# A fused attention, soft mixture and gated mixture: the second mixture's tiles laid out anew, its first loads in the other order, the last expert's additions on another engine

## The chip, the core and the metric

One core of a Trainium2 chip runs the whole program in one launch. The engines work side by side, each through its own queue in order: TensorE (PE, with PEld for its weight loads), VectorE (DVE), ScalarE (ACT) and GpSimd (POOL); SyncE (SP) issues the DMAs. The metric is the device time in microseconds (us); lower is better. TensorE runs at one of two granted clocks, 1.2 or 2.4 GHz, and the profile gives the granted share (0.5 or 1.0).

## The reference

```python
x = attn(q, k, v, M_prev, z_prev, beta)        # (2304, 512): local causal softmax mixed with a memory read
# first mixture: 8 experts, 4 slots each
d = softmax(x @ phi, axis=0); slots = d.T @ x
for e in range(8): slot_out[e] = relu(slots[e] @ w1[e]) @ w2[e]
x = softmax(x @ phi, axis=1) @ slot_out         # c @ slot_out, rank 32
# second mixture: 8 experts over all 2304 rows
P = exp(x @ w_gate - max); 8 times: P /= rows' sums, P /= columns' sums, P *= N / 8
out = sum over e of P[:, e:e+1] * (relu(x @ w1[e]) @ w2[e])
```

All inputs and outputs are float32.

## The kernel before

Attention runs first (its pairs of heads one after another), with the routing of the first mixture beside it. The first mixture follows (lines 762 to 861): its 32 weight pieces `wm` of 1 MB each are loaded by SP into ten `big`, four `bg2` and eight `wb` buffers; PE multiplies the slots with them (line 830, layer 1; line 848, layer 2, into `pso`), and lines 854 to 860 copy and turn `pso` into `soT`, the 32 slot outputs. `hT` is the hidden layer that line 848 reads as weights of PE.

The second mixture never forms x. x is `c @ slot_out`, so the first layer of expert e becomes `c4T` (the combine weights, times P for that expert) times `A_e = slot_out @ w1[e]`. `prepare_a` (line 986) makes A from the loaded `w1`; `split_a` cuts it into a rounded part `ahi` and a remainder `alo`; `spread_a` (line 1009) multiplies these by the selection matrix `sel` so that each slot row stands where the 128-row layer-1 matmul wants it; `store_a` writes the result to `a4`. Every product of the second mixture is done in three matmuls, high by high, high by low and low by high, to keep float32 accuracy.

The rows are cut into nine units of 256, so that there are 72 steps: eight experts of nine units. The first six units of expert 0 are multiplied in the plain way (`plain`, line 1316: 128x512 matmuls). All other 66 steps use seven products instead of eight on 2x2 blocks (Winograd's form): line 1344, `product`, each of 12 matmuls of 128x256, in the order p5, p1, p7, p6, p2, p3, p4. In a product the hidden tile (`a11h`, `s1l`, ...) is loaded as PE's weights and the weight tile (`BB1h`, `T2l`, ...) streams past it. The two combined hidden tiles come from DVE (line 1059), ACT rounds them (line 1065), POOL or DVE makes the remainders (lines 1076, 1072). DVE adds the products from PSUM into `accA`, `accB`, `accD` (line 1370). `layer1` (line 1030, eight matmuls, `l<-c4T,a`) of the next unit stands between the second product and the third; its PSUM banks are free when DVE has read `a22l` of the unit before (line 1072).

For each expert the weights are prepared beside the products of the expert before (`w_sum`, `w_hi`, `w_lo`, lines 936 to 968). For expert 0 that happens ahead: `load_w1(0, 1)` and then `load_raw(0)` (lines 1400, 1401) queue four 0.5 MB loads each on SP, and in the stretch with a written order (lines 1411 on) ACT rounds the raw second layer to `BB1h`, `BB2h` and POOL makes `BB1l`, `BB2l`; then come `prepare_a`, `gate_slots` (which repeats `soT` four times into `soB` for the gate), `split_a`, `spread_a`, `store_a`, `layer1`. `sel` is made by a DVE `tensor_scalar` (line 972) and three DVE casts of `ident` (line 978); these stand outside the written order and are placed by the scheduler.

At the last expert `add_u` (line 1252) adds the shared part U, kept in `accA[:, :256]`, to `accB` and `accD`, both on DVE, right behind the collection of p2; each finished block is sent out by SP as soon as it is final.

The tiles are laid one after another in the order in which they are first asked for, each rounded up to 32 bytes, pool behind pool: `mA`, `mB`, `mC`, `mD`. Counted from the first byte of `mA` and taken by 512 bytes, which is where `c4T` starts too, the tiles begin at:

| tile | before | after the change |
|---|---|---|
| BB1, T1 and T2 of even experts, c4T | 0 | 0 |
| T1, T2 of odd experts, T4, BB2, raw | 192 | 0 |
| a11, a12, a22, a21 and s3 (one tile) | 64 | 64 |
| s1, s2, s4 | 192 | 64 |
| a4 | 160 | 64 |

`rr` (72 bytes) and `cs` (32) stand ahead of `cP`, `chi`, `f` and `s1`, `s2`, `s4` in `mB`; that is where the 128 bytes between 64 and 192 come from. `sel` at the start of `mD` lies over the second `hT`, whose last reader is the last matmul of line 848.

Of the kernel before, what the change touches and what calls it, by code (L numbers as in the profile page):

```python
# [8 lines left out]
F32 = mybir.dt.float32  # L9
BF16 = mybir.dt.bfloat16  # L10
F32R = mybir.dt.float32r
AF = mybir.ActivationFunctionType
# [9 lines left out]
def infini_attention_soft_moe_sinkhorn_moe(  # L22
# [848 lines left out]

    mA = ctx.enter_context(tc.tile_pool(name="mA", bufs=1, reuse_waits="tile"))
    mB = ctx.enter_context(tc.tile_pool(name="mB", bufs=1, reuse_waits="tile"))
    mC = ctx.enter_context(tc.tile_pool(name="mC", bufs=1, reuse_waits="tile"))
    mD = ctx.enter_context(tc.tile_pool(name="mD", bufs=1, reuse_waits="tile"))
    ps_l = ctx.enter_context(tc.tile_pool(name="ps_l", bufs=1, space=PSUM, reuse_waits="tile"))
# [91 lines left out]
        )  # L968


    sel = mD.tile([P, 4, 160], F32R, name="sel")
    nc.vector.tensor_scalar(
        out=sel.rearrange("p j c -> p (j c)"), in0=ones[:, 0:1].to_broadcast([P, 640]),
# [2 lines left out]
    for r in (0, 2, 4):  # L976
# [1 line left out]
        nc.vector.tensor_copy(  # L978
            sel[:, :, 32 * r : 32 * r + 32], ident.rearrange("p (j s) -> p j s", j=4)
        )  # L980
    a2s, a4s, G = {}, {}, {}

    def aux(nm):
        return ps_a.tile([P, 512], F32, tag="a", name=nm)
# [13 lines left out]
    def split_a(e):  # L998
        pa = a2s[e]
        ahi = mB.tile([P, 256], F32R, tag="ahi", name="ahi")  # L1000
        nc.scalar.activation(out=ahi, in_=pa[:, 0:256], func=AF.Copy)
        alo = mB.tile([P, 256], F32R, tag="alo", name="alo")
        nc.vector.tensor_tensor(
            out=alo, in0=pa[:, 0:256], in1=ahi.bitcast(F32), op=ALU.subtract
        )
        a2s[e] = ahi, alo
        a4s[e] = mD.tile([P, FF], F32R, tag="a4", name="a4", bufs=2)

    def spread_a(e, n):

# [97 lines left out]

    soR = soT.rearrange("p c (o s) -> p c o s", o=1)
    Pr = mB.tile([P, NTT, E], F32, name="Pr")  # L1110
    Cw = mD.tile([P, NTT, NS], F32, name="Cw")

    gsel = mD.tile([P, E + NS], F32R, name="gsel")
    m1 = mD.tile([P, 1], F32, name="m1")
    m2 = mD.tile([1, 1], F32, name="m2")

    def gate_slots():
        soB = G["soB"] = mB.tile([P, KD, 4, NS], F32, tag="c4", name="soB")
        for c in range(KD):
            nc.vector.tensor_copy(soB[:, c], soR[:, c].to_broadcast([P, 4, NS]))  # L1120

    def gate_weights():
        pg, soB = aux("pg"), G["soB"]
# [46 lines left out]
        nc.scalar.activation(out=Pr, in_=Pr, func=AF.Exp, bias=m1)  # L1170

    def balance_rows():
        rr = mB.tile([P, NTT], F32, tag="rr", name="rr")
        nc.vector.tensor_reduce(out=rr, in_=Pr, op=ALU.add, axis=AX.X)
        nc.vector.tensor_scalar_add(rr, rr, 1e-9)
        nc.vector.reciprocal(rr, rr)
        nc.vector.tensor_tensor(
            out=Pr, in0=Pr, in1=rr.rearrange("p (t o) -> p t o", o=1).to_broadcast([P, NTT, E]),
            op=ALU.mult,
        )  # L1180
        cs = G["cs"] = mB.tile([P, E], F32, tag="cs", name="cs")
        nc.vector.tensor_reduce(
            out=cs, in_=Pr.rearrange("p t e -> p e t"), op=ALU.add, axis=AX.X
        )
# [67 lines left out]
    def add_u(u, g):  # L1252

        A, B_, D_ = accA[:, u], accB[:, u], accD[:, u]
        eng(g[0]).tensor_tensor(
            out=halves(B_), in0=halves(B_), in1=both(A[:, 0:CW]), op=ALU.add
        )
        eng(g[1]).tensor_tensor(out=D_, in0=D_, in1=A[:, 0:CW], op=ALU.add)
# [100 lines left out]
    def collect(g, k, y):  # L1359
        e, u = units[g]  # L1360
        nm = ORDER[k]

        A, B_, D_ = accA[:, u], accB[:, u], accD[:, u]
        new, end = e == 0, e == E - 1

        def put(acc, y, new=new):
            if new:
                nc.scalar.activation(out=acc, in_=y, func=AF.Copy)
            else:
                nc.vector.tensor_tensor(out=acc, in0=acc, in1=y, op=ALU.add)  # L1370

        def send(i, c, t):
            r0 = P * (2 * u + i)
            nc.sync.dma_start(out[r0 : r0 + P, CW * c : CW * c + CW], t)

        if nm == "p5":
            put(halves(B_), both(y))
        elif nm == "p1" and e == 1 and u < RAW:
            put(A[:, 0:CW], y, True)
            put(A[:, CW:], y)  # L1380
        elif nm == "p1":
            put(halves(A), both(y))
        elif nm == "p7":
            put(D_, y)
        elif nm == "p2":
            put(A, Y[g, "y3"], False)
            if end:
                send(0, 0, A[:, CW:])
                add_u(u, "DD")
        elif nm == "p3":  # L1390
            put(B_, Y[g, "y2"], False)
            if end:
                send(0, 1, B_[:, 0:CW])
                send(1, 1, B_[:, CW:])
        elif nm == "p4":
            put(D_, y, False)
            if end:
                send(1, 0, D_)

    load_w1(0, 1)  # L1400
    load_raw(0)
    BB.update({(2, z): mC.tile([P, KH, 2, CW], F32R, name=f"BB2{z}") for z in "hl"})
    EX = {}

# [5 lines left out]
    with tc.manual_schedule(engines={E_.PE, E_.DVE, E_.Activation, E_.Pool}):  # L1410
        for nm in ("B11", "B12", "B21", "B22"):
            for i in range(2):
                w_hi(0, nm, i)
                w_lo(0, nm, i, "P")
        prepare_a(0)
        gate_slots()
        split_a(0)
        spread_a(0, 0)
        spread_a(0, 1)
        store_a(0, 0)  # L1420
        store_a(0, 1)
        layer1(0)
        split_h(0, "a11")
        split_h(0, "a21")
        gate_weights()
        for g in range(len(units)):
            nxt = g + 1 < len(units)
            for k in range(7):
                s = 7 * g + k
                if g < RAW:  # L1430
                    plain(g, k)
                    if k == 3:
                        layer1(g + 1)
                    if k == 0:
                        if g:
                            store(g - 1, 2)
                        split_h(g, "a12")
                    elif k == 1:
                        split_h(g, "a22")
                    elif k == 6:  # L1440
                        store(g, 1)
                    if k > 3 and g == RAW - 1:
                        hidden(g + 1, k - 2)
                    elif k in (4, 5):
                        split_h(g + 1, ("a11", "a21")[k - 4])
                else:

                    EX[s + 1] = g, k, product(g, k)
                    if k == 1 and nxt:
                        layer1(g + 1)  # L1450
                    if g == RAW and k == 0:
                        store(g - 1, 2)
                        hidden(g, 5)
                        hidden(g, 6)
                    if k not in (3, 4):
                        result(s)
                    if k == 0:
                        hidden(g, 0)
                    elif k > 1 and nxt:
                        hidden(g + 1, k)  # L1460
                    result(s)
                for fn, args in side.pop(s, ()):
                    fn(*args)
        result(7 * len(units))
# [60 lines left out]
```

## Time and profile before

| | |
|---|---|
| device time, median of three runs | 1181.48 us (1179.54 to 1184.17) |
| profiled execution | 1182.51 us, of which the span from the first to the last instruction is 1180.7 us |
| busy | PE 1120.1 us (95%), DVE 865.7 (73%), ACT 656.3 (56%), POOL 641.8 (54%) |
| attention, first mixture, second mixture | 0 to 268 us, 268 to 316, 316 to the end |
| mean granted clock | 0.986 |

In the profile a line gives start, duration, engine, source line, operation, output<-inputs, shapes and, in brackets, how long the engine was idle before and who ended it. A PE matmul's own duration holds its way through the array; what one costs in a dense stream is the distance from its start to the next start.

### The profile page before, as it was taken

How to read it: one execution, taken by the hardware profiler on the slowest of the kernel's cores; microseconds unless marked ns; L12 is line 12 of the kernel's file. 1: busy time of each engine (PE TensorE's matmuls, PEld its weight loads, DVE VectorE, ACT ScalarE, POOL GpSimd, SP SyncE). 2: the span in 40 equal slices, each digit the busy share in tenths (PEclk: the TensorE clock that was granted, in tenths of full speed). 3: DMA queues.
4: the chain of work that ended last, by engine and by line, in shares of the span. 5: the costliest groups of instructions: out<-in, count | busy, mean ns of one | idle time of the engine just before them, and what ended most of it. 6: DMA issues, size and time to landing. Idle time of an engine off the chain costs nothing.

```text
span 1180.7 us, 24363 instructions
## 1 busy us (share of the span) xinstructions
PE 1120.1 (95%) x9247; PEld 1018.6 (86%) x9247; DVE 865.7 (73%) x1891; ACT 656.3 (56%) x1422; POOL 641.8 (54%) x585
## 2 busy tenths in 40 slices
PE   6899999979799999999999999999999999999998
PEld 4677777764287888999999999999999999999998
DVE  6888888874337566677778767777876777788886
ACT  6788888741233487546545644654564465456342
POOL 5433323200323297577677767767776776686443
PEclk9999999998989999999999999999999999999999
DMA  6677686249702004002100400210040031000111
GB/s 158 192 200 226 197 245 178 74 187 376 309 6 71 1 2 143 1 2 82 62 2 1 143 2 1 92 53 1 1 143 1 2 108 37 2 1 19 42 50 54
DMA packets 37412, 102.32 MB, mean 87 GB/s; under 512 B 6448, under 2 KB 13232, under 8 KB 33200
## 3 DMA queue, kind: packets, MB, share of 16 engines
q1 hardware_dynamic: 36864, 100.69, 26.5%
q8 instruction: 73, 1.20, 0.4%
q14 instruction: 43, 0.35, 0.1%
q10 hardware_dynamic: 432, 0.09, 0.0%
HBM read 96.04 MB, written 4.72 MB: 85 GB/s over the span
## 4 chain that ended last, share of the span: by engine, by line
PE 75%; DVE 11%; ACT 7%; DMA 3%; issue 2%; POOL 1%; SPq 0%; ACTq 0%; DVEq 0%; POOLq 0%
PE y L1356 16%; PE y L1354 16%; PE y L1355 16%; PE l L1035 6%; PE y L1321 5%; PE po L436 3%; PE pt L399 2%; ACT sm L360 2%; DMA wm<-in_moe_w_dram 1%; PE pa L992 1%; DVE sm L356 1%; PE pc L1221 1%; PE ph L830 1%; DVE f L1059 1%; DMA raw<-in_moe_w_dram 1%
## 5 line engine op out<-in xcount | busy, mean ns | idle before, releaser
L1059 DVE SCALAR_TENSOR_TENSOR f<-l,f 128x512 f32<-128x512 f32 x264 | 181.4, 687 | 56.6 <-ACT a11h L1065 44.4
L1076 POOL TENSOR_TENSOR s1l<-f,s1h 128x512 fp32r<-128x512 f32 x66 | 88.4, 1340 | 170.0 <-ACT s1h L1065 165.9
L1370 DVE TENSOR_TENSOR accA<-accA,y 128x512 f32<-128x512 f32 (+1 forms) x129 | 86.6, 671 | 57.1 <-PE y L1356 51.6
L1065 ACT ACTIVATE a12h<-l 128x512 fp32r<-128x512 f32 x72 | 43.1, 598 | 121.6 <-DVE f L1059 121.6
L1076 POOL TENSOR_TENSOR s4l<-f,s4h 128x512 fp32r<-128x512 f32 x66 | 86.0, 1303 | 39.9 <-ACT s4h L1065 39.8
L1370 DVE TENSOR_TENSOR accB<-accB,y 128x512 f32<-128x512 f32 x129 | 88.3, 684 | 13.7 <-PE y L1356 2.3
L1035 PE MATMUL l<-c4T,a 128*128 128x256 f32 x576 | 82.7, 286 | 9.2 <-DVE a22l L1072 8.3
L1076 POOL TENSOR_TENSOR s2l<-f,s2h 128x512 fp32r<-128x512 f32 x66 | 85.9, 1301 | 0.8 <-ACT s2h L1065 0.8
L1076 POOL TENSOR_TENSOR s3l<-f,s3h 128x512 fp32r<-128x512 f32 x66 | 86.0, 1303 | 0.3 <-ACT s3h L1065 0.3
L1035 PEld LDWEIGHTS l<-c4T,a 128*128 128x128 f32 x576 | 75.0, 190 | 12.4 <-DVE a22l L1072 10.8
L360 ACT ACTIVATE sm<-sm,mn 128x128 f32<-128x128 f32 (+3 forms) x128 | 71.1, 556 | 19.5 <-DVE mn L356 17.9
L965 POOL TENSOR_TENSOR BB1l<-raw,BB1h 128x512 fp32r<-128x512 f32 x32 | 41.0, 1293 | 68.9 <-ACT BB1h L959 68.9
L1354 PE MATMUL y<-T2h,s2h 128*128 128x256 f32 x264 | 76.9, 291 | 0.0
L1354 PE MATMUL y<-BB2h,a12h 128*128 128x256 f32 x264 | 75.0, 284 | 0.0
L1355 PE MATMUL y<-BB2l,s4h 128*128 128x256 f32 x264 | 74.6, 283 | 0.1
L1354 PE MATMUL y<-BB1h,a11h 128*128 128x256 f32 x264 | 73.4, 278 | 1.3 <-DVE accB L1370 1.3
L1356 PE MATMUL y<-T4h,a22l 128*128 128x256 f32 x264 | 74.6, 283 | 0.0
L1356 PE MATMUL y<-BB2h,a12l 128*128 128x256 f32 x264 | 74.5, 282 | 0.0
L1356 PE MATMUL y<-BB2h,s4l 128*128 128x256 f32 x264 | 74.5, 282 | 0.0
L1354 PE MATMUL y<-BB2h,s4h 128*128 128x256 f32 x264 | 74.5, 282 | 0.0
L1354 PE MATMUL y<-T4h,a22h 128*128 128x256 f32 x264 | 74.3, 281 | 0.0
L1356 PE MATMUL y<-T1h,s1l 128*128 128x256 f32 x264 | 74.1, 281 | 0.0
(313 smaller groups left out, 4219.0 us busy)
## 6 DMA issues: line engine op xcount, KB each, us to landing
wm<-in_moe_w_dram SPq DMA_DIRECT2D x32, 1024.0 KB, 7.7
w<-in_moe_w_dram SPq DMA_DIRECT2D x32, 512.0 KB, 4.4
raw<-in_moe_w_dram SPq DMA_DIRECT2D x32, 512.0 KB, 4.1
qd<-in_q_dram SPq DMA_DIRECT2D x30, 288.0 KB, 4.2
kd<-in_k_dram SPq DMA_DIRECT2D x30, 288.0 KB, 4.5
qp<-in_q_dram SPq DMA_DIRECT2D x16, 288.0 KB, 3.4
vt<-in_v_dram SPq DMA_DIRECT2D x16, 256.0 KB, 2.7
out_dram<-accB SPq DMA_DIRECT2D x18, 128.0 KB, 1.8
```

What stands on the lines that cost most here:

```text
L360: nc.scalar.activation(out=sm[:, 0:n], in_=sm[:, 0:n], func=AF.Exp, scale=-1.0, bias=mnc, accum_out=X.sums[:, i, h : h + 1],)
L436: nc.tensor.matmul(po[64 * h : 64 * h + 64, c0:w], X.vt[:, j, h, :], rhs, start=(j == 0), stop=(j == n - 1),)
L965: eng(g).tensor_tensor(out=w_tile(e, nm, "l")[:, h], in0=full(e, nm, i), in1=w_tile(e, nm, "h")[:, h].bitcast(F32), op=ALU.subtract,)
L1035: nc.tensor.matmul(ph[:, f, :], a4s[e][:, P * (KH * j + f) : P * (KH * j + f) + P], c4T[:, UT * u : UT * u + UT], start=True, stop=True,)
L1059: nc.vector.scalar_tensor_tensor(out=f_tile(g, nm), in0=ph(g, src), scalar=0.0, in1=b, op0=ALU.max, op1=op)
L1065: nc.scalar.activation(out=h_tile(g, nm, "h"), in_=ph(g, nm) if a else FU[g, nm], func=AF.Relu if a else AF.Copy)
L1076: nc.gpsimd.tensor_tensor(out=lo, in0=FU[g, nm], in1=hi, op=ALU.subtract)
L1321: nc.tensor.matmul(Y[g, i], X[g, f"a{i}{j}", "hhl"[n]][:, f, :], BB[j, "hlh"[n]][:, f].rearrange("p a c -> p (a c)"), start=j == 1 and f = ...
L1354: nc.tensor.matmul(o_, hh[:, f, :], wh[:, f, :], start=f == 0, stop=False)
L1355: nc.tensor.matmul(o_, hh[:, f, :], wl[:, f, :], start=False, stop=False)
L1356: nc.tensor.matmul(o_, hl[:, f, :], wh[:, f, :], start=False, stop=f == KH - 1)
L1370: nc.vector.tensor_tensor(out=acc, in0=acc, in1=y, op=ALU.add)
```

## The change

```diff
+    mS = ctx.enter_context(tc.tile_pool(name="mS", bufs=1, reuse_waits="tile"))
+    mS.tile([P, 24], F32, name="gap")
     mC = ctx.enter_context(tc.tile_pool(name="mC", bufs=1, reuse_waits="tile"))
...
+    mD.tile([P, 16], F32, name="gap")
+    a4s = {0: mD.tile([P, FF], F32R, tag="a4", name="a4", bufs=2)}
+    Cw = mD.tile([P, NTT, NS], F32, name="Cw")
     sel = mD.tile([P, 4, 160], F32R, name="sel")
...
-    gsel = mD.tile([P, E + NS], F32R, name="gsel")
-    m1 = mD.tile([P, 1], F32, name="m1")
-    m2 = mD.tile([1, 1], F32, name="m2")
+    gsel = mS.tile([P, E + NS], F32R, name="gsel")
+    m1 = mS.tile([P, 1], F32, name="m1")
+    m2 = mS.tile([1, 1], F32, name="m2")
...
-        for c in range(KD):
-            nc.vector.tensor_copy(soB[:, c], soR[:, c].to_broadcast([P, 4, NS]))
+        nc.scalar.activation(out=soB, in_=soR.to_broadcast([P, KD, 4, NS]), func=AF.Copy)
...
-        rr = mB.tile([P, NTT], F32, tag="rr", name="rr")
+        rr = mS.tile([P, NTT], F32, tag="rr", name="rr")
...
-        cs = G["cs"] = mB.tile([P, E], F32, tag="cs", name="cs")
+        cs = G["cs"] = mS.tile([P, E], F32, tag="cs", name="cs")
...
             if end:
                 send(0, 0, A[:, CW:])
-                add_u(u, "DD")
+                if u == NU - 1:
+                    add_u(u, "DP")
         elif nm == "p3":
             put(B_, Y[g, "y2"], False)
-            if end:
+            if end and u == NU - 1:
                 send(0, 1, B_[:, 0:CW])
                 send(1, 1, B_[:, CW:])
         elif nm == "p4":
             put(D_, y, False)
             if end:
+                if u < NU - 1:
+                    add_u(u, "PP")
+                    send(0, 1, B_[:, 0:CW])
+                    send(1, 1, B_[:, CW:])
                 send(1, 0, D_)
 
+    load_raw(0)
     load_w1(0, 1)
-    load_raw(0)
...
         prepare_a(0)
-        gate_slots()
         split_a(0)
         spread_a(0, 0)
         spread_a(0, 1)
         store_a(0, 0)
         store_a(0, 1)
+        gate_slots()
         layer1(0)
```

`rr` and `cs` leave `mB`, and the small pool `mS` (448 bytes) stands between `mB` and `mC`, which gives the third column of the table above. `sel` moves to the end of `mD`, above everything that the first mixture uses. `raw` takes the places that expert 0's `w1` had, and the other way round. In `add_u` the letters are the engines of the addition into `accB` and of that into `accD`: D for DVE, P for POOL. For the first eight units of the last expert both additions stand on POOL behind the collection of p4, and the three blocks are sent there; the ninth keeps its place behind p2, with the second addition on POOL.

## Rows read from the trace of the kernel before

**Rows 1.** Waits of TensorE, 427 to 1181 us: total, times, longest.
```profile
PE l L1035 <- DVE a22l L1072: 7.8, 10, 1.7
```
**Rows 2.** The same view, 470 to 1082 us: the whole answer.
```profile
PE pa L992 <- ACT c4T L1226: 0.2, 1, 0.2
```
**Rows 3.** The waits of all engines, 1082 to 1166 us, the last expert.
```profile
PE l L1035 <- DVE a22l L1072: 3.7, 7, 0.6
PE y L1354 <- DVE accB L1370: 1.3, 1, 1.3
```
**Rows 4.** Timeline of PE, one unit of expert 5: each product's first matmul.
```profile
913.81 0.28 PE L1354 MATMUL y<-T1h,s1h 128*128 128x256 f32 x1
...
917.58 0.28 PE L1354 MATMUL y<-BB1h,s3h 128*128 128x256 f32 x1
918.96 0.28 PE L1354 MATMUL y<-T2h,s2h 128*128 128x256 f32 x1
920.40 0.28 PE L1354 MATMUL y<-BB2h,a12h 128*128 128x256 f32 x1
...
924.68 0.28 PE L1354 MATMUL y<-T1h,s1h 128*128 128x256 f32 x1
```
**Rows 5.** The same, one unit of expert 6.
```profile
1016.31 0.28 PE L1354 MATMUL y<-T1h,s1h 128*128 128x256 f32 x1
...
1021.43 0.28 PE L1354 MATMUL y<-T2h,s2h 128*128 128x256 f32 x1
...
1022.79 0.28 PE L1354 MATMUL y<-BB2h,a12h 128*128 128x256 f32 x1
...
1027.08 0.28 PE L1354 MATMUL y<-T1h,s1h 128*128 128x256 f32 x1
```
**Rows 6.** Timeline of DVE in the unit of rows 4.
```profile
914.60 0.69 DVE L1072 SCALAR_TENSOR_TENSOR a22l<-l,a22h 128x512 fp32r<-128x512 f32 x1 [0.17 <-ACT a22h L1065]
```
**Rows 7.** Timeline of DVE where the second mixture starts.
```profile
316.12 1.41 DVE L972 TENSOR_SCALAR sel<-ones 128x640 fp32r<-128x640 f32 x1
...
318.66 3.74 DVE L978 CAST sel<-ident 128x128 fp32r<-128x128 f32 x3
...
323.81 0.41 DVE L1003 TENSOR_TENSOR alo<-pa,ahi 128x256 fp32r<-128x256 f32 x1
```
**Rows 8.** Timelines of SP's queue, ACT and POOL ahead of that.
```profile
295.72 4.53 SPq L922 DMA_DIRECT2D w<-in_moe_w_dram  x4
300.30 5.14 SPq L915 DMA_DIRECT2D raw<-in_moe_w_dram  x4
...
311.48 2.42 ACT L959 ACTIVATE BB1h<-raw 128x512 fp32r<-128x512 f32 x4 [13.61 <-DMA raw<-in_moe_w_dram]
312.19 4.99 POOL L965 TENSOR_TENSOR BB1l<-raw,BB1h 128x512 fp32r<-128x512 f32 x4 [40.87 <-ACT BB1h L959]
317.14 5.17 POOL L965 TENSOR_TENSOR BB2l<-raw,BB2h 128x512 fp32r<-128x512 f32 x4
318.33 0.38 ACT L1001 ACTIVATE ahi<-pa 128x256 fp32r<-128x256 f32 x1 [1.95 <-PE pa L992]
```
**Rows 9.** Timeline of PE in the same place.
```profile
324.28 0.58 PE L1017 MATMUL p<-ahi,sel 128*128 128x256 f32 x1 [6.09 <-DVE alo L1003]
...
330.57 0.77 PE L1321 MATMUL y<-BB1h,a11h 128*128 128x512 f32 x1
```
**Rows 10.** Sums by stretch: us, PE, PEld, DVE, ACT, POOL busy, PEclk, DMA share, GB/s.
```profile
316.00:336.00 20.00, 12.87 (x77) 10.84 (x78) 12.46 (x19) 3.77 (x9) 7.53 (x6) 0.66 0.29 105
```
**Rows 11.** Timeline of PE, last expert: the first matmul of two units.
```profile
1108.25 0.28 PE L1354 MATMUL y<-T1h,s1h 128*128 128x256 f32 x1
...
1119.89 0.28 PE L1354 MATMUL y<-T1h,s1h 128*128 128x256 f32 x1
```
**Rows 12.** DVE by line, 1082 to 1166 us: busy, mean ns, idle before.
```profile
L1255 DVE TENSOR_TENSOR accB<-accB,accA 128x512 f32<-128x512 f32 x8 | 12.3, 1536 | 0.3
```
**Rows 13.** Timeline of DVE, the last unit.
```profile
1174.32 0.69 DVE L1255 TENSOR_TENSOR accB<-accB,accA 128x512 f32<-128x512 f32 x1
```

More of the change, by code (lines that the diff above doesn't have):

```diff
@@ L980, in infini_attention_soft_moe_sinkhorn_moe @@
         )
-    a2s, a4s, G = {}, {}, {}
+    a2s, G = {}, {}
     def aux(nm):
@@ L1006, in split_a @@
         a2s[e] = ahi, alo
-        a4s[e] = mD.tile([P, FF], F32R, tag="a4", name="a4", bufs=2)
+        if e:
+            a4s[e] = mD.tile([P, FF], F32R, tag="a4", name="a4", bufs=2)
     def spread_a(e, n):
@@ L1110, in infini_attention_soft_moe_sinkhorn_moe @@
     Pr = mB.tile([P, NTT, E], F32, name="Pr")
-    Cw = mD.tile([P, NTT, NS], F32, name="Cw")
-    gsel = mD.tile([P, E + NS], F32R, name="gsel")
-    m1 = mD.tile([P, 1], F32, name="m1")
-    m2 = mD.tile([1, 1], F32, name="m2")
+    gsel = mS.tile([P, E + NS], F32R, name="gsel")
+    m1 = mS.tile([P, 1], F32, name="m1")
+    m2 = mS.tile([1, 1], F32, name="m2")
     def gate_slots():
         soB = G["soB"] = mB.tile([P, KD, 4, NS], F32, tag="c4", name="soB")
-        for c in range(KD):
-            nc.vector.tensor_copy(soB[:, c], soR[:, c].to_broadcast([P, 4, NS]))
+        nc.scalar.activation(out=soB, in_=soR.to_broadcast([P, KD, 4, NS]), func=AF.Copy)
     def gate_weights():
```

## The prediction

> **What bounds the kernel now.** I read four views in this order: the waits of TensorE, the starts of its matmuls in two units, the timelines where the second mixture begins, and the last expert by line.
>
> The waits come first, because they say where a faster TensorE is worth anything. From 470 to 1082 us TensorE waits 0.2 us in all [rows 2]: 53 units run at the pace of its own instructions. The 7.8 us that it waits for DVE's `a22l` from 427 us on [rows 1] lie elsewhere: 3.7 us in the last expert [rows 3], the other 4.1 in the first Winograd units ahead of 470, where units are held up by other engines.
>
> Inside the dense stretch the matmuls don't all cost the same. In the unit of expert 5, p7 takes 918.96 - 917.58 = 1.38 us, 115 ns for each of its 12 matmuls; p6 takes 1.44 (120 ns), and p2, p3 and p4 take 924.68 - 920.40 = 4.28, 119 ns each; the unit takes 10.87 us [rows 4]. In expert 6 p6 takes only 1.36 us, 113.3 ns each, while the three last products stay at 119; the unit takes 10.77 [rows 5]. Same shapes, same engine, same place in the unit: between the two experts only the place of T2 differs. By the table of tile starts, weights and stream of p7 lie 64 bytes apart by 512 (`s3` against BB1). p6 of expert 5 has 0 apart (`s2` and T2 both at 192), p6 of expert 6 has 192 apart. p2 and p4 stand at 64 against 192, p3 at 0. So the distance between the two operands that TensorE reads at the same time, the next weights and the current stream, moves a 256-column matmul between 113 and 120 ns.
>
> At the start of the second mixture TensorE stands idle 6.09 us for `alo` [rows 9]. DVE is busy from 316.12 to 323.81 with `sel` and `soB`; three casts of 128x128 take 3.74 us, 1.25 each [rows 7], and POOL's remainders beside them also take 1.25 each (4.99 / 4) [rows 8]: each cast waits out one POOL instruction. The granted clock then averages 0.66 over 20 us [rows 10]; between its two levels that is 20 x 0.34 / 0.5 = 13.6 us at 1.2 GHz, behind that idle time.
>
> The Trainium skill has this in SBUF — State Buffer, section "SBUF: two separate sides": VectorE and GpSimd share a port pair as "an exclusive lock", and the loser blocks for a whole instruction. The casts at POOL's own 1.25 us agree [rows 7, 8].
>
> **The change part by part.** All sums are made against the profiled execution, 1182.5 us, which is 1.0 above the median of 1181.5.
>
> *Tile places.* After the change every product and layer 1 reads weights at 64 and stream at 0: p1 and p7 have exactly these places now, and the other five products and layer 1 join them. A unit without side work has 84 product matmuls and 8 of layer 1. At 113.3 ns that is 10.42 us, at 115 it is 10.58; since the first matmuls behind a change of tile are some ns slower, I take 10.51. From 10.87 (odd experts) that saves 0.36, from 10.77 (even ones) 0.26. The units that profit are 11 to 71, 34 of odd and 27 of even experts: 34 x 0.36 + 27 x 0.26 = 19.3 us; I take 19. Bounds: with 10.58, 34 x 0.29 + 27 x 0.19 = 15; with 10.42, 25. Units 6 to 10 get nothing, since others hold them up. The 128x512 matmuls of the first six units change places too (`a12`, `a22` against BB2): 6 x 24 of them, and at 6.7 ns (120 - 113.3) either way that is 1 us up or down, taken at 0.
>
> What is late next, when the unit shrinks: layer 1 waits for `a22l`. In the unit of rows 4 it ends at 915.29 [rows 6], and layer 1 begins 8 matmuls ahead of 917.58, at 916.6: 1.3 us to spare. As both `a22l` and layer 1 follow p4's end of the unit before, only the 24 matmuls between get shorter, 0.1 us or so. The cover holds.
>
> *sel, soB and the order of the loads.* `alo` needs `ahi`, which ends at 318.71 [rows 8], and 0.41 us of DVE [rows 7]: 319.1, so that the first matmul on it can start at 319.2 in place of 324.28 [rows 9]. For that DVE must be free at 318.7. `sel` no longer lies over `hT`, and so can be made while DVE and POOL are idle during the first mixture. `soB` leaves DVE. Raw moves ahead by the place of four loads, 300.30 - 295.72 = 4.6 us in SP's queue, so `BB1h` starts near 307, and POOL's ten us end near 317.5 in place of 322.3 [rows 8]. So even a `sel` that stayed where it is would meet one POOL instruction. Taken: 5.1 us. `w1` now lands where raw landed. ACT was through with the last of raw at 318.33 - 1.95 = 316.4 [rows 8], two roundings of 0.6 behind its landing near 315.2; `pa` begins near 316.3. The margin is one us, and what `w1` is late beyond it comes off the gain. `soB` on ACT, one instruction of 512 elements, costs about what a `BB1h` does (2.42 / 4 = 0.6 us), behind `store_a`, while TensorE runs layer 1, for which ACT has to wait anyway.
>
> The half-clock stretch: TensorE is busy 12.87 us of these 20 [rows 10]; some 3 lie at the full clock, so at most half of 10, 4.9 us, come back if the clock stays up. If it falls all the same, a little later, 13.6 us of dense work run at half pace, and lose 6.8 where 4.9 were lost: 2 us worse. What decides is whether the two shorter pauses that stay, 1 us for `alo` and 1 us for `a4`, still pull it down; I count 1 us of gain. This part: 6, from 3 to 10.
>
> *The last expert.* Its unit takes 1119.89 - 1108.25 = 11.64 us [rows 11] against 10.87 of the other odd experts. DVE adds into `accB` with 1.54 us on average [rows 12], and with 0.69 at the end, where POOL has nothing left [rows 13]. That, and the smaller addition into `accD`, stands ahead of s4's sum, whose chain ends in `a22l`, for which TensorE waits in each of the seven units [rows 3]. With both on POOL DVE does what it does in the other experts, with 1.3 us to spare. Saved: 6 x 0.77 = 4.6, and in the unit at 1083 us, the longest, the 1.3 us for `accB` [rows 3] and its own 0.77: 6.7. On POOL the additions (1.3 us, as a remainder, and half) stand ahead of `s4l`. Two us late there are covered, because `s4l` is wanted by the third matmul of p3, with five products ahead of it (5 x 1.38 us). The sends of B come half a unit later, on a queue that has nothing else to do; only the ninth unit's reach the end, and these stay. Bounds: 5 to 7.
>
> By the same lock of the skill's SBUF page, the ninth unit's additions (one on each engine at once) exclude each other: up to 0.7 us later, with p3 and p4 of TensorE beside it. No run here shows that pair.
>
> Sum: 19 + 6 + 6.7 = 31.7; 1182.5 - 31.7 = 1150.8, 1150 on the scale of the median.
>
> **Rivals.**
>
> *Places don't matter.* p1 and p7 could be fast for where they stand in the unit. Then the 19 us are missing: 1182.5 - 12.7 = 1169.8, 1169 on the median's scale. Against it speaks p6 at 120 and 113 ns in the same place [rows 4, 5]; for it, that p5 and layer 1 are slow in both.
>
> This is also what the Trainium skill makes one expect, in TensorE: Matmul & The Clock Gate, "Step-by-step: what each phase is for": two independent read ports, and "Loading the next tile's weights doesn't steal SBUF read bandwidth from the running matmul". The p6 pair disagrees with that [rows 4, 5].
>
> *Another engine takes over.* The other engines' work per unit stays the same while the unit shrinks by 3%. If DVE's or POOL's queue falls behind where an expert's weights are prepared, half of the 19 us go into waits: 1160. Against it stands the 1.3 us to spare; for it, that this margin is from a unit with little side work.
>
> *The other side.* The new common distance is bad where the tiles alternate: TensorE reads three streams of one product in turn, now all at the same place by 512. At the start part's 6 and the last expert's 6.7, the 61 x 92 = 5612 matmuls decide: if each gets 2.3 ns slower than the 118 ns of today's mean (10.87 / 92), 12.7 us are eaten and the kernel is slower; at 5 ns it is 15 us slower, 1198. No row shows a dense product above 120 ns, and p7 runs at these very places.
>
> *The change doesn't do what it says*: `sel` stays late. As worked out above, that costs under a us.
>
> **Chances.** Forecast (1140 to 1157) 0.70, another engine 0.12 (1157 to 1165), places don't matter 0.12 (1165 to 1172), the other side 0.03, the rest below 1140. The range, 1140 to 1165, reaches down to the greatest gain of every term (25 + 10 + 7 = 42) and holds the first two cases. Against 1181.5 no change means 1176 to 1187, 0.5%, about what a measurement of this kernel can tell from none: 0.95 faster, 0.02 the same, 0.03 slower.
>
> **What would show it.** Starts of p6, p2, p3 and p4 1.36 to 1.38 us apart in every expert, and a unit of 10.5 us in odd and even experts alike. The first matmul on `ahi` within 1.2 us of the end of `pa`, and no DVE copy there above 0.5 us. No wait for `a22l` in the last expert, and its units as long as the others'. The prediction is wrong if the products stay at 119 ns, if waits of TensorE for POOL or DVE show between 470 and 1082 us, or if `pa` waits for its load.

## The result and the profile after

The changed kernel takes 1151.9 us (median of 4 runs, 1148.5 to 1156.5) where the kernel before, beside it, takes 1181.6: ratio 0.975, 95% interval 0.971 to 0.979, faster. The forecast was 1150, from 1140 to 1165. Its profiled execution took 1150.5 us, 32.0 less than the profiled execution before. By stage, in us, the two traces differ as follows; the other rows are the experiments told below, each in one profiled execution of its own. The columns: from the end of the first mixture (start of the last copy into `soT`) to TensorE's first matmul on `ahi`; from there to the first Winograd unit (6); units 11 to 62; from unit 63 to the end, which is the last expert; the execution's time. Units 6 to 10 take 65.7 to 65.9 in all of them.

```
                        pause  first   11-62   last   time
before                   8.30   91.6   589.9  109.1  1182.5
after                    3.25   88.3   575.2  100.8  1150.5
tile places alone        8.47   91.4   583.0  108.4  1175.1
all but places           3.25   88.4   593.9  100.9  1170.4
additions on DVE         3.25   88.3   579.5  108.2  1162.2
common distance 0        3.38   87.6   605.1  103.3  1181.7
w1 first                 5.09   93.1   577.0   97.9  1156.7
soB on DVE               3.26   88.3   574.8   97.9  1148.3
after, once more         3.25   90.3   577.7  100.9  1155.5
low parts 128 further    3.25   88.1   574.4   97.9  1146.5
```

So the 32.0 are 5.0 of pause, 3.3 behind it, 14.7 in units 11 to 62, 8.3 in the last expert, and 0.7 ahead of and between these. The timeline of PE of the kernel after, one unit of expert 5, the first matmul of p5, p7, p6, p2 and of the next p5 (start, duration, engine, line, operation, tiles, shape), answers to [rows 4]:

```profile
904.61 0.28 PE L1360 MATMUL y<-T1h,s1h 128*128 128x256 f32 x1
...
908.24 0.28 PE L1360 MATMUL y<-BB1h,s3h 128*128 128x256 f32 x1
...
909.60 0.28 PE L1360 MATMUL y<-T2h,s2h 128*128 128x256 f32 x1
...
910.96 0.28 PE L1360 MATMUL y<-BB2h,a12h 128*128 128x256 f32 x1
...
915.04 0.28 PE L1360 MATMUL y<-T1h,s1h 128*128 128x256 f32 x1
```

p7 and p6 take 1.36 us each and the last three products 4.08, 113.3 ns a matmul; the unit takes 10.43 us, and so do units with the same work in expert 6, where [rows 5] had 10.77. The last expert's unit, which answers to [rows 11], is another matter:

```profile
1081.23 0.28 PE L1360 MATMUL y<-T1h,s1h 128*128 128x256 f32 x1
...
1092.07 0.28 PE L1360 MATMUL y<-T1h,s1h 128*128 128x256 f32 x1
```

10.84 us with the same 92 matmuls, at the same tile places. It isn't a wait: the waits of PE (total, times, longest) are these, the only ones from 470 to 1059 us, where [rows 2] had 0.2 in all and none for `a22l`, and from 1059 to the end, where [rows 3] had 3.7 for `a22l` and 1.3 for `accB`:

```profile
PE l L1043 <- DVE a22l L1080: 0.8, 5, 0.2
...
PE l L1043 <- DVE a22l L1080: 0.2, 1, 0.2
```

Each of its matmuls is 118 ns after the one before (10.84 us / 92). Where the second mixture starts, timelines of DVE, POOL and PE and the sums of one stretch answer to [rows 7 to 10]:

```profile
315.58 0.49 DVE L979 TENSOR_SCALAR sel<-ones 128x640 fp32r<-128x640 f32 x1
316.10 1.46 DVE L985 CAST sel<-ident 128x128 fp32r<-128x128 f32 x3
318.21 0.42 DVE L1010 TENSOR_TENSOR alo<-pa,ahi 128x256 fp32r<-128x256 f32 x1 [0.65 <-ACT ahi L1008]
...
305.80 4.99 POOL L969 TENSOR_TENSOR BB1l<-raw,BB1h 128x512 fp32r<-128x512 f32 x4 [36.10 <-ACT BB1h L963]
310.75 4.97 POOL L969 TENSOR_TENSOR BB2l<-raw,BB2h 128x512 fp32r<-128x512 f32 x4
315.67 1.54 POOL L960 TENSOR_TENSOR ft<-raw,raw 128x512 f32<-128x512 f32 x1
...
318.69 0.39 PE L1025 MATMUL p<-ahi,sel 128*128 128x256 f32 x1 [1.04 <-DVE alo L1010]
```
```profile
316.00:336.00 20.00, 17.53 (x123) 13.90 (x116) 7.81 (x18) 6.93 (x15) 3.79 (x3) 1.00 0.30 106
```

POOL is through with its eight remainders at 315.7, `sel` is still made behind `soT` and meets one POOL instruction (the one at 315.67), DVE then waits 0.65 us for ACT, and the clock stays at the higher of its two levels, 2.4 GHz (1.00).

### The profile page after: what moved, and what is told of

Same layout as the page of the kernel before. It is cut to its first block, busy times and chain, and to the rows that moved or that the text cites. A ratio compares the mean times of both kernels' runs of the same rounds, so it can differ in the third digit from the quotient of the medians.

```text
span 1148.7 us, 24354 instructions
## 1 busy us (share of the span) xinstructions
PE 1096.2 (95%) x9247; PEld 992.6 (86%) x9247; DVE 853.0 (74%) x1870; ACT 656.6 (57%) x1423; POOL 658.7 (57%) x602
## 4 chain that ended last, share of the span: by engine, by line
PE 71%; DVE 13%; ACT 9%; issue 3%; DMA 2%; POOL 2%; SPq 0%; DVEq 0%; ACTq 0%; POOLq 0%
PE y L1360 15%; PE y L1362 15%; PE y L1361 15%; PE y L1327 5%; PE l L1043 5%; PE po L436 3%; DVE f L1067 2%; PE ph L830 2%; ACT sm L360 2%; PE pt L399 1%; PE pa L999 1%; DVE sm L356 1%; DMA kd<-in_k_dram 1%; DVE a22l L1080 1%; PE pc L1227 1%
## 5 line engine op out<-in xcount | busy, mean ns | idle before, releaser
L1043 PE MATMUL l<-c4T,a 128*128 128x256 f32 x576 | 79.0, 280 | 7.5 <-DVE a22l L1080 6.6
L1043 PEld LDWEIGHTS l<-c4T,a 128*128 128x128 f32 x576 | 71.6, 188 | 10.4 <-DVE a22l L1080 8.8
L1063 ACT ACTIVATE f<-l 128x512 f32<-128x512 f32 x66 | 39.1, 592 | 65.3 <-PE l L1043 61.9
L1362 PE MATMUL y<-BB1h,s3l 128*128 128x256 f32 x264 | 73.3, 278 | 0.1
L1361 PE MATMUL y<-T2l,s2h 128*128 128x256 f32 x264 | 73.4, 278 | 0.0
L1362 PE MATMUL y<-T2h,s2l 128*128 128x256 f32 x264 | 73.3, 278 | 0.0
L1361 PE MATMUL y<-T4l,a22h 128*128 128x256 f32 x264 | 73.2, 277 | 0.0
```

What stands on the lines that cost most here:

```text
L1043: nc.tensor.matmul(ph[:, f, :], a4s[e][:, P * (KH * j + f) : P * (KH * j + f) + P], c4T[:, UT * u : UT * u + UT], start=True, stop=True,)
L1063: nc.scalar.activation(out=f_tile(g, nm), in_=ph(g, nm), func=AF.Relu)
L1361: nc.tensor.matmul(o_, hh[:, f, :], wl[:, f, :], start=False, stop=False)
L1362: nc.tensor.matmul(o_, hl[:, f, :], wh[:, f, :], start=False, stop=f == KH - 1)
```

## The experiments

**TensorE alone, sixteen distances.** The distance is that from the stream's address to the weights' address in a partition; "by 256" (or 512) is what is left of it when whole multiples of 256 (512) bytes are taken off. The inner loops of the kernel:

```
for w in ws:                      # the weights 0, 32, ... 480 bytes past the stream by 512
    for width in (256, 40, 128, 200):
        kick(width)               # one matmul of that width
        # 3 times: 4 x (w.hi | mh), (w.hi | ml), (w.lo | mh), 128x256
```

> Leaves out the whole computation: TensorE alone runs dense 128x256 products of the same form as the kernel's (two streams, weights in eight slices), with the weights 0, 32, 64 ... 480 bytes past the stream by 512, 144 matmuls at each distance, in four blocks that begin behind a matmul of another width. Theory (the distance between the next weights and the current stream sets the pace): 113 to 114 ns from start to start at 64, 119 to 120 at 0 and at 384, about 118 at 160, 113 or 117.5 at 192. Rival, places don't matter: one pace within 1 ns at all sixteen distances. Rival, the slow pace is other engines reaching into the same memory: one pace at all sixteen, and that 113 or less, since no other engine runs beside it.

Measured, median ns from start to start in the four blocks; at 256 to 480 bytes the same again, within 1 ns:

```
  0: 120 120 120 120    32: 117 117 117 117    64: 113 118 113 113    96: 120 119 119 117
128: 119 119 119 119   160: 119 119 119 119   192: 118 118 118 118   224: 117 118 117 117
```

Timeline of PE in it, blocks 1 and 2 at 64 bytes (`wC`) and block 1 at 0 (`wA`), each time the fourth matmul and the 34th, 30 apart:

```profile
52.67 0.28 PE L67 MATMUL y<-mh,wC 128*128 128x256 f32 x1
...
56.07 0.28 PE L67 MATMUL y<-mh,wC 128*128 128x256 f32 x1
...
56.87 0.28 PE L67 MATMUL y<-mh,wC 128*128 128x256 f32 x1
...
60.40 0.28 PE L67 MATMUL y<-mh,wC 128*128 128x256 f32 x1
```
```profile
17.47 0.28 PE L67 MATMUL y<-mh,wA 128*128 128x256 f32 x1
...
21.07 0.28 PE L67 MATMUL y<-mh,wA 128*128 128x256 f32 x1
```

3.40 and 3.53 us at one distance, 113.3 and 117.7 ns, and 3.60 (120 ns) at the other. The distance sets the pace with no other engine at work, it repeats after 256 bytes and not 512, and at 64 there are two steady paces: the block behind a matmul of 40 columns falls into the slow one and stays there. The rivals, one pace at all distances, fall. By the Trainium skill, TensorE: Matmul & The Clock Gate, "Step-by-step: what each phase is for", loading the next weights takes nothing from the running matmul, and all of these would be equal; they are not, by up to 7 ns of 113.

**The tile places alone.** From the kernel after, the rest undone (`gate_slots` is called ahead of `split_a` again):

```
-    load_raw(0)
     load_w1(0, 1)
+    load_raw(0)
...
-        nc.scalar.activation(out=soB, in_=soR.to_broadcast([P, KD, 4, NS]), func=AF.Copy)
+        for c in range(KD):
+            nc.vector.tensor_copy(soB[:, c], soR[:, c].to_broadcast([P, 4, NS]))
...
                 send(0, 0, A[:, CW:])
-                if u == NU - 1:
-                    add_u(u, "DP")
+                add_u(u, "DD")
```

> The kernel after with the order of loads, the copies of soB on DVE and the last expert's additions put back as before: only the tile places are left. Theory: 14.7 us in units 11 to 62 as the two traces have it, and some 3 in the last expert, 1181.5 - 17.5 = 1164, ratio 0.985 (prediction's own term: 19, from 15 to 25). TensorE's pause for alo (6.1 us), the half-clock stretch and the wait for a22l in the last expert stay. Rival, places don't matter: 1181, ratio 1.000. Rival, another engine takes over: 1170 or more, with waits of TensorE in units 11 to 62.

Measured: 1171.1 us (1166.3 to 1175.1), ratio 0.989 (0.984 to 0.994): a gain clear of the noise, but 7 us less than expected. By its time alone this could be the rival "another engine takes over" (1170 or more), but that had waits of TensorE in units 11 to 62, and they come to 0.5 us. Its timeline of PE has both paces, a unit of expert 5 and a unit of expert 6:

```profile
909.12 0.28 PE L1361 MATMUL y<-T1h,s1h 128*128 128x256 f32 x1
...
919.55 0.28 PE L1361 MATMUL y<-T1h,s1h 128*128 128x256 f32 x1
...
1009.84 0.28 PE L1361 MATMUL y<-T1h,s1h 128*128 128x256 f32 x1
...
1020.67 0.28 PE L1361 MATMUL y<-T1h,s1h 128*128 128x256 f32 x1
```

10.43 and 10.83 us. Experts 1 and 5 run at 113 ns, experts 2, 3, 4 and 6 at 118; each keeps its pace through its undisturbed units. Units 11 to 62 take 583.0, 7.8 more than in the kernel after, where experts 1 to 6 are all fast: 2 us for each slow expert. So in this layout the gain of the places is not one number but depends on how many experts an execution catches in the slow pace.

**All but the places.** The kernel before, with the three other edits (`gate_slots` behind `store_a`, `collect` as in the kernel after):

```
-    load_w1(0, 1)
     load_raw(0)
+    load_w1(0, 1)
...
-        for c in range(KD):
-            nc.vector.tensor_copy(soB[:, c], soR[:, c].to_broadcast([P, 4, NS]))
+        nc.scalar.activation(out=soB, in_=soR.to_broadcast([P, KD, 4, NS]), func=AF.Copy)
...
+                if u < NU - 1:
+                    add_u(u, "PP")
```

> The kernel before with raw loaded first, soB in one ACT instruction behind store_a, and the last expert's additions on GpSimd; tile places as before. Theory: start 5 us of pause and 3.3 of clock, last expert some 6: 1181.5 - 14.5 = 1167, ratio 0.988; products of units 11 to 62 at 10.8 to 10.9 us a unit as before. If the clock falls at the start all the same, 1170. Rival, places don't matter: 1150 to 1152, as the whole change.

Measured: 1171.0 us (1170.4 to 1171.6), ratio 0.990 (0.987 to 0.993). The pause, the clock and the last expert are those of the kernel after, the units those of the kernel before, as expected. 4 us are missing in units 11 to 62, 593.9 against 589.9, nearly all in one unit. Timelines of DVE, POOL and PE there:

```profile
759.16 4.03 DVE L1205 TENSOR_TENSOR cP<-Cw,Pr 128x128 f32<-128x128 f32 x1
...
758.01 1.33 POOL L1076 TENSOR_TENSOR s3l<-f,s3h 128x512 fp32r<-128x512 f32 x1
759.27 1.31 POOL L1076 TENSOR_TENSOR s4l<-f,s4h 128x512 fp32r<-128x512 f32 x1
760.51 2.53 POOL L965 TENSOR_TENSOR BB2l<-raw,BB2h 128x512 fp32r<-128x512 f32 x2
...
764.20 0.63 PE L1220 MATMUL pc<-ident,c 128*128 128x128 f32 x4 [2.37 <-DVE c L1215]
```

The product for `cP`, 0.30 us in the same place before, takes 4.03: it ends with POOL's chain of back-to-back instructions, at 763.0 (763.2). By the Trainium skill, SBUF — State Buffer, "SBUF: two separate sides", the loser of the shared ports blocks for the winner's whole instruction; here it outlasted three. An unbroken chain on POOL does not always do this: in the kernel before, POOL runs from 758.4 to 772.5 us without a break, and the product at 767.1 takes 0.30. So one unit out of 61 loses about 4 us to another engine, as in the rival "another engine takes over", though here the units had not shrunk. It shows in this kernel and in the one at distance 0 (3.99); in the two profiled executions of the kernel after the longest such product takes 1.40 and 2.45.

**The additions back on DVE.** The kernel after, with both additions behind p2 in every unit, and the sends of B behind p3:

```
         elif nm == "p4":
-                if u < NU - 1:
-                    add_u(u, "PP")
-                    send(0, 1, B_[:, 0:CW])
-                    send(1, 1, B_[:, CW:])
```

> The kernel after with the last expert's two additions back on DVE behind p2, and the sends with them. Theory: TensorE waits again for a22l in seven units, the last expert's unit takes 11.2 to 11.6 us in place of 10.84, and the unit at its begin some 1.5 us more: 1151.5 + 5 = 1156 to 1158. Rival, the additions on GpSimd brought nothing, since the 118 ns from matmul to matmul that the last expert shows after the change comes from them (GpSimd beside TensorE): units of the last expert then have their products at 113 ns, and the waits for a22l only use up what that gives: 1151 to 1153.

Measured: 1164.2 us (1162.2 to 1165.7), ratio 0.984 (0.981 to 0.988), 12 above the kernel after, more than either reading had. From unit 63 on the trace has 108.2 in place of 100.8, 7.4 us more. Another 4.3 lie in units 11 to 62, where experts 1 and 6 ran at 118 ns in this execution. Waits of all engines in its last expert, and from its timeline of PE a p5 and the layer 1 behind it:

```profile
PE l L1043 <- DVE a22l L1080: 3.9, 7, 0.6
...
PE y L1360 <- DVE accB L1376: 1.7, 1, 1.7
```
```profile
1100.50 0.28 PE L1360 MATMUL y<-T1h,s1h 128*128 128x256 f32 x1
...
1103.99 1.19 PE L1043 MATMUL l<-c4T,a 128*128 128x256 f32 x8 [0.50 <-DVE a22l L1080]
```

The waits of [rows 3] are back, at the new places. They do more than cost their own time. The p5 shown takes 1.41 us, at 118 ns; the p7 behind this layer 1 takes 1.36, at 113. In the next unit it is 118 again, and so on: units 65 to 70 take 11.54, 11.90, 11.32, 11.90, 11.34 and 11.92 us. Each time the pace turns at an interruption, at the wait for `a22l` or, once, at a break of 0.2 us ahead of p1; in the kernel after, with a single such wait of 0.2 us in its last expert, unit after unit stays at 118. As three of these units run for the most part at 113, some 260 matmuls in all, the additions cost about 1 us more than the 7.4 (an estimate, 260 x 4.5 ns). The rival, that GpSimd's additions make the 118 ns, falls with the other experts: these show 118 with no such additions.

**A common distance of 0.** The kernel after, with `Pr` moved and `a4` put ahead of its gap, so that weights and streams stand at the same place:

```
+    a4s = {0: mD.tile([P, FF], F32R, tag="a4", name="a4", bufs=2)}
     mD.tile([P, 16], F32, name="gap")
-    a4s = {0: mD.tile([P, FF], F32R, tag="a4", name="a4", bufs=2)}
...
-    Pr = mB.tile([P, NTT, E], F32, name="Pr")
+    Pr = mS.tile([P, NTT, E], F32, name="Pr")
```

> The kernel after with all products and layer 1 on one common distance of 0 instead of 64 (gate tile moved, so that weights and streams stand at the same place by 512); all else as after. Theory: 120 ns for every 256-column matmul in every expert, an undisturbed unit 11.0 to 11.1 us, units 11 to 62 about 575 + 4850 x 6.6 ns = 607 us, in all 1186 to 1190, slower than before by some 0.5%, and with less spread from run to run, as there is no second pace. Rival, the gain came from one common place for all products whatever it is: 1151, as after.

Measured: 1180.9 us (10 runs, 1177.8 to 1185.1), ratio 0.998 (0.997 to 1.000). An undisturbed unit of expert 5:

```profile
915.86 0.28 PE L1360 MATMUL y<-T1h,s1h 128*128 128x256 f32 x1
...
926.90 0.28 PE L1360 MATMUL y<-T1h,s1h 128*128 128x256 f32 x1
```

11.04 us, 120 ns, in every expert; units 11 to 62 take 605.1 where 607 was expected. The distance does in the kernel what it does alone. A wrong one eats all that the rest of the change gives, so the prediction's rival on the other side was a real danger, if a little short of slower. The total was expected 5 us too high, because I added the difference in the last expert too, which had been at 118 ns already. Against what was expected the spread did not shrink; it goes at least in part with the granted clock (0.988 in the two slowest runs, 1183.5 and 1185.1, and 0.990 to 0.993 in the others).

**w1 first, and soB on DVE.** Two kernels, each the kernel after with one edit of the start undone, the first and the second part of this diff (in the second `gate_slots` stands ahead of `split_a` again):

```
-    load_raw(0)
     load_w1(0, 1)
+    load_raw(0)
...
-        nc.scalar.activation(out=soB, in_=soR.to_broadcast([P, KD, 4, NS]), func=AF.Copy)
+        for c in range(KD):
+            nc.vector.tensor_copy(soB[:, c], soR[:, c].to_broadcast([P, 4, NS]))
```

> The kernel after with w1 loaded ahead of raw as before; all else as after. Theory: POOL's remainders run 4.6 us later beside the sel casts on DVE, which take 1.25 each; ahi ends near 318.7 and alo waits for DVE, so that TensorE's first matmul on alo starts at 320 to 321 in place of 318.7: 2 us dearer; if the clock falls at that pause, 3 more. Rival, the order of the loads is what took away all of the 5 us: first matmul near 324. Rival, it did nothing, soB alone did it: 319.

> The kernel after with soB made by four DVE copies ahead of alo, as before; raw stays first. Theory: POOL is through when the copies run, so that they and the sel casts take 0.2 to 0.5 us each; first matmul on alo at 319.5 to 320.5 in place of 318.7, 1 to 1.5 us dearer. Rival, soB's move alone took away the pause: first matmul at 322 or later.

Timelines of DVE and PE and the sums of the stretch, with w1 first:

```profile
317.31 3.63 DVE L985 CAST sel<-ident 128x128 fp32r<-128x128 f32 x3
320.86 0.41 DVE L1010 TENSOR_TENSOR alo<-pa,ahi 128x256 fp32r<-128x256 f32 x1
...
321.32 0.39 PE L1025 MATMUL p<-ahi,sel 128*128 128x256 f32 x1 [2.88 <-DVE alo L1010]
```
```profile
316.00:336.00 20.00, 15.95 (x86) 13.12 (x85) 9.25 (x15) 4.86 (x10) 8.07 (x7) 0.66 0.29 105
```

and with `soB` on DVE and raw first:

```profile
317.62 0.49 DVE L1127 COPY soB<-soT 128x128 f32<-128x128 f32 x3
319.32 0.42 DVE L1010 TENSOR_TENSOR alo<-pa,ahi 128x256 fp32r<-128x256 f32 x1 [1.20 <-ACT ahi L1008]
...
319.80 0.39 PE L1025 MATMUL p<-ahi,sel 128*128 128x256 f32 x1 [1.04 <-DVE alo L1010]
```

With w1 first the casts wait out POOL again, the pause is 1.8 us longer, the clock falls to 1.2 GHz for some of the stretch (mean 0.66), and the stretch behind it takes 4.8 us more: 6.6 in all. With `soB` on DVE and raw first nothing is lost, where 1 to 1.5 us had been expected: each copy takes 0.16 us with POOL through, and DVE still waits for ACT. The order of the loads alone brings the whole of this part. `soB` on ACT without it brings 8.47 - 5.09 = 3.4 of the 5.2 us of pause between the kernel with the places alone and the kernel after, and nothing of the clock. Each of the two ran once; but in the table every execution with raw first has a pause of 3.25 to 3.38, and every one with w1 first 5.09 or more.

**Four operands.** TensorE alone again, with the two weight tiles apart from each other and the two streams too.

```
# a, b, c each of 0, 64, 128, 192 bytes past wh by 256; entries of 256, 40, 128, 200, 88 columns
# 2 times: 4 x (hh at a | wh), (hh at a | wl at c), (hl at b | wh)
```

> Leaves out the whole computation: TensorE alone. The two weight tiles and one of the two streams stand 0, 64, 128 or 192 bytes past the other stream by 256, in all 64 combinations, each entered behind a matmul of 256, 40, 128, 200 and 88 columns and run for 24 matmuls; then all weights 40 to 112 past the streams in steps of 8; then at 64 a block entered behind 40 columns (118 ns), an inserted matmul of 16 to 256 columns, and a second block. Theory (distance by 256 and, at 64, the phase at entry): 113 ns only with both weights 64 past both streams, from most entries and not from that of 40 columns; every other combination 116 to 121; some inserted widths turn 118 into 113. Rival, the pace depends on what ran before and not on the places: the five entries differ in the same way in all combinations. Open: whether one combination gives 113 or less from every entry.

Measured, mean ns of the last 12 matmuls for the five entries, some of the 64 combinations (high weights, low weights, low stream):

```
 64  64   0:  113.3 117.8 113.3 113.3 117.8
 64 192   0:  113.3 113.3 113.3 113.3 113.3
192  64   0:  113.3 113.3 113.3 113.3 113.3
 64 128 128:  115.5 115.6 115.6 115.5 115.6
  0   0   0:  120.1 120.0 120.0 120.0 120.0
```

The means over the entries of all others lie between 115.6 and 120.3. Expected was 113 with both weights at 64 alone; that the low parts at 192 bring it from every entry was open. Timeline of PE at entry 40, first 64/64/0 and then 64/192/0: the small matmul, the 13th behind it, and the next small one, 12 further:

```profile
321.51 0.18 PE L47 MATMUL kick<-wh,hh 128*128 128x40 f32 x1
...
323.04 0.28 PE L60 MATMUL y<-wh,hh 128*128 128x256 f32 x1
...
324.45 0.22 PE L47 MATMUL kick<-wh,hh 128*128 128x128 f32 x1
...
438.74 0.18 PE L47 MATMUL kick<-wh,hh 128*128 128x40 f32 x1
...
440.23 0.28 PE L60 MATMUL y<-wh,hh 128*128 128x256 f32 x1
...
441.59 0.22 PE L47 MATMUL kick<-wh,hh 128*128 128x128 f32 x1
```

1.41 us and 1.36. In the last part, inserted matmuls of 64, 128 and 192 columns turned 118 into 113, and those of 16, 48 and 96 turned 113 into 118; behind the six other widths 118 stayed 118. The block behind 40 columns, which had 118 above, began three times out of twelve at 113. So neither the places nor the width of the last matmul settle it, but what ran before does; I call this the phase. What sets it where an expert of the kernel begins was not tested. With all weights at 56 or 72 bytes no entry got below 117.8; at 88 three of five got to 113.3.

**The low parts 128 bytes further.** The combination 64/192/0 in the kernel after, and that kernel unchanged beside it:

```
+    mL = ctx.enter_context(tc.tile_pool(name="mL", bufs=1, reuse_waits="tile"))
+    mL.tile([P, 32], F32, name="gap")
     mS = ctx.enter_context(tc.tile_pool(name="mS", bufs=1, reuse_waits="tile"))
-    mS.tile([P, 24], F32, name="gap")
+    mS.tile([P, 56], F32, name="gap")
...
-            X[g, nm, z] = mB.tile([P, KH, P], F32R, tag=tag, name=nm + z)
+            pool = mL if z == "l" else mB
+            X[g, nm, z] = pool.tile([P, KH, P], F32R, tag=tag, name=nm + z)
```

> The kernel after, with the low parts of the hidden tiles (the third matmul's weights in every product) 128 bytes further by 256: high parts 64 and low parts 192 past the streams, the combination that ran at 113.3 ns from all five entries when TensorE ran alone. Theory (two paces at 64, chosen by the phase in which an expert begins): one pace is left, every undisturbed unit of experts 1 to 7 takes 10.43 us, units 11 to 62 take 575, the last expert's units 10.43; 1146 to 1148, and the runs lie within 3 us of each other. Rival, something in the last expert or in an expert's preparation sets the 118 ns: units of 10.84 remain and the runs spread as those of the kernel after, median 1150 to 1153. Rival, the places interact with other engines here: slower than after.

> The kernel after, unchanged, on the same chip beside it. Theory: each execution has its own experts at 10.43 and at 10.84 us a unit, at about 2 us (2.6 for the last expert) for each expert at the slower pace; runs from 1146 to 1160, median 1150 to 1153, and in the profile not the same experts slow as before. Rival, the slow last expert is a property of its code: again expert 7 alone at 10.84.

Measured: 1147.8 us (6 runs, 1146.1 to 1153.4), ratio to before 0.969 (0.966 to 0.973), against 1155.7 (1151.2 to 1158.8), 0.975 (0.971 to 0.979), of the unchanged kernel: 7.9 us between the medians, though the two intervals just overlap. The second gap grows so that the tiles behind it keep their places by 256. A unit of the last expert of the new kernel, and then, of the unchanged one, a unit of expert 1 and one of the last:

```profile
1079.67 0.28 PE L1363 MATMUL y<-T1h,s1h 128*128 128x256 f32 x1
...
1090.10 0.28 PE L1363 MATMUL y<-T1h,s1h 128*128 128x256 f32 x1
```
```profile
497.24 0.28 PE L1360 MATMUL y<-T1h,s1h 128*128 128x256 f32 x1
...
508.08 0.28 PE L1360 MATMUL y<-T1h,s1h 128*128 128x256 f32 x1
...
1086.22 0.28 PE L1360 MATMUL y<-T1h,s1h 128*128 128x256 f32 x1
...
1097.05 0.28 PE L1360 MATMUL y<-T1h,s1h 128*128 128x256 f32 x1
```

10.43 in the one, in all seven experts; 10.84 in the other in expert 1, which had been fast in its first profile, and again in the last. That the last expert was slow in both makes it likelier to be caught, but not bound to: with w1 first, or `soB` on DVE, the same code took 10.43 there. The new kernel's median lies under both medians of the unchanged one, 1151.9 and 1155.7; that it has one pace is read from its one profile and the five entries above; its five other runs have no profile. Its runs spread more than expected, and by the clock: four runs with a mean granted clock of 0.989 to 0.991 lie between 1146.1 and 1149.0, two with 0.986 at 1153.0 and 1153.4. The unchanged kernel's profile shows where that comes from, in the sums of the stretch behind the pause, the clock being the third number from the end:

```profile
316.00:336.00 20.00, 18.02 (x112) 15.16 (x113) 7.46 (x17) 5.31 (x12) 4.55 (x4) 0.83 0.29 106
```

The same pause of 1.04 us, and the clock fell all the same: 6.8 of these 20 us are at 1.2 GHz (20 x 0.17 / 0.5), and the stretch takes 2 us more.

## Why the prediction was right, point by point

The total came out within 2 us, and in that there is luck. In the profiled execution the places gave 4.3 us less than forecast (14.7 for 19, just under the bound of 15), the start 2.3 more (8.3 for 6) and the last expert 1.6 more (8.3 for 6.7, over the bound of 7), and these nearly cancel. The three mechanisms were right in the main; what the first lacked is the second pace.

*Tile places*, 19 us from 15 to 25. The mechanism was right: alone, in the kernel, and against a distance of 0. In the profiled execution after the change the stretch from unit 11 to 62 gave 14.7; the last expert's share was missing. I took 10.51 us for every unit from 11 on; there is no such unit, only 10.43 and 10.84 where nothing else is done. By the kernel with the low parts moved, which has one pace, the full term is 589.9 - 574.4 = 15.5, and 100.9 - 97.9 = 3.0 in the last expert against the kernel with all but the places: 18.5. So 19 was the size of the term at its best, but again by two errors that cancel: with 10.43 put for all 61 units my sum gives 24 (34 x 0.44 + 27 x 0.34), and 5 or 6 of these don't come, because units with side work gain less. In expert 5 the second unit, where the next expert's A is made, takes 13.74 us in that kernel and 13.65 before, the first and the eighth 11.07 and 11.04 for 11.31. What an execution gets of the term is less by 2 us for each of experts 1 to 6 that is caught at 118 ns, and by 3 for the last. The start-up loss that I read from p7's 115 ns in [rows 4] was there (its matmuls follow at 120, 114, 124 and 118 ns, and then at 113); after the change, with layer 1 ahead of it at the same distance, p7 has 113 throughout.

*The distance rule itself* was read off one pair, p6 at 0 and at 192 [rows 4, 5]. Alone, 192 runs at 118 and not at 113; why p6 of expert 6 was fast there, behind p7 at 64, is open. The distance counts by 256 bytes, not 512.

*Start*, 6 us from 3 to 10: 5.0 of pause as worked out (5.1), and 3.3 of clock, where I counted 1. The clock stayed up in the first profile; in the second it fell, which cost 2 us: the term is 8.3 or 6.3. I had `sel` moving into DVE's idle time; it did not move, and that cost nothing, as the rival said. What freed DVE is raw's place ahead of w1, of which POOL's earlier end is the effect.

*The last expert*, 6.7 us from 5 to 7: 7.4, by the kernel with the additions back on DVE, and 109.1 - 100.9 = 8.2 at the old places. Of the 8.2, 1.1 lie behind the last matmul (4.6 us from its start to the end before, 3.5 with the additions on POOL, but 3.9 and 3.7 in the two other kernels that keep them on DVE), where I counted nothing; that leaves about 7. The waits for `a22l` went, 3.7 to 0.2 [rows 3]. One sign that I named did not come: its units are not as long as the others', 10.84 against 10.43, which is the second pace again. These are the additions as lines of POOL there (count, total busy, mean ns, idle before):

```profile
L1261 POOL TENSOR_TENSOR accB<-accB,accA 128x512 f32<-128x512 f32 x8 | 10.3, 1292 | 2.5 <-DVE accB L1376 2.5
L1264 POOL TENSOR_TENSOR accD<-accD,accA 128x256 f32<-128x256 f32 x7 | 5.1, 733 | 0.0
```

1.29 and 0.73 us, for which 1.3 and half of it had been taken; TensorE waits 0.2 us in all there. In the ninth unit, where the two additions start together, POOL's takes 1.24 us in place of 0.73: 0.5 later, within the 0.7 that I had allowed.

*The rivals.* "Places don't matter" fell twice, with TensorE alone and in the kernel at distance 0. "Another engine takes over" did not decide the kernel after: its waits of TensorE for DVE between 470 and 1059 us, which I had named as a sign of being wrong, come to 0.8 us; a loss of 4 us to another engine showed in two of the experiments. "The other side" needs a distance such as 0.

## What to carry to other kernels

Where dense 256-column matmuls set the time, read their starts one by one: a spacing that changes with the tile and not with the work is worth a test of the operands' distance, by 256 bytes here, with all weights and streams varied. If a kernel has runs some us apart, look whether its stages run at one of two paces; a layout that has only the fast one is worth more than one that reaches it now and then. Where an elementwise engine stalls beside GpSimd, moving the load that GpSimd waits for can do what moving the stalled work would.

## What was not expected of the hardware

- Two steady paces of TensorE, 113.3 and 117.8 ns, at the same addresses, the same shapes and full clock; a matmul of another width can turn one into the other, in either direction. With the two weight tiles at 64 and at 192 bytes past the streams only the fast one was seen.
- In a kernel, interruptions of 0.2 to 0.8 us turned one pace into the other, in one expert from unit to unit.
- A vector operation of 0.30 us took 4.03 beside three GpSimd instructions in a row, and 0.30 beside a row as unbroken.
- The granted clock behind one and the same pause of 1.04 us averaged 1.00 over 20 us in one execution and 0.83 in another.
